# A nested Strassen–Winograd kernel on one core: PSUM as two tiles of two adjacent banks, and sums of seven blocks handled as wide operations

## The chip, the core and the metric

The kernel runs on one core of a Trainium2 chip. Its engines work side by side, each through its own instructions in order: TensorE (PE, matmuls, with the loading of the stationary operand shown apart as PEld), VectorE (DVE), ScalarE (ACT), GpSimd (POOL) and SyncE (SP, which here only issues DMAs). Matmuls write to PSUM, of which the kernel uses eight banks of 512 float32 numbers for each of 128 partitions. The metric is device time in microseconds (us), lower is better; 747.59 us is the median before the change.

## What is computed

Normalised linear attention in eight batches of eight heads, and a feed-forward block on its output:

```python
kv = np.einsum('bhsd,bhse->bhde', k, v)          # batch 8, heads 8, seq 576, head_dim 64
out = np.einsum('bhsd,bhde->bhse', q, kv)
rms = np.sqrt(np.mean(out * out, axis=-1, keepdims=True) + 1e-06)
attn = out / rms * g_norm
x = attn.transpose(0, 2, 1, 3).reshape(4608, 512)
a = x @ w1                                       # 512 x 1024
b = x @ w2
h = a * b @ w3                                   # 1024 x 1024
return h @ w_out                                 # 1024 x 512
```

## The kernel before

**Stages.** First w3 and w_out are multiplied into one 1024 x 512 matrix (`fold_chunk`, L678, four PSUM banks for a half), while weights arrive as 64-bit numbers and are turned into float32 (`conversion`). Then tokens are worked through in nine groups of 512: 512 tokens of a batch each, and one group (T = 8) of the 64 tokens left over from every batch; the order is T = 0 to 6, 8, 7. For a group there are the *gates* (x @ w1 and x @ w2, multiplied elementwise) and the *projection* by the folded matrix. The attention of batch T + 1 runs in pieces between products of group T: `between()` takes the next piece of `steps(b)`, which has eight lists of calls, and two `between()` are in each call of the gates, two in each half of the blocks. Where a piece has matmuls they are kv products (`begin_kv`, L335), the products with q (`finish` → `product`, L413, followed by `norm`, L374) and `product_left` (L432).

**Strassen–Winograd.** A product of 2 x 2 blocks is made with seven block products and some sums. `winograd` (L696) issues them in the order p1 (a11·b11), p5 (s1·t1), s2·t2 onto p1's bank (giving u2), s4·b22 onto p5's bank, s3·t3 onto the first bank (u3), a12·b21 into a third bank, a22·t4 onto the first. So three banks, r1, r2 and r3, serve seven products. What is needed later is kept in SBUF by a copy on ACT (`keep`, L717 to L719: p1, p5, u2, sometimes u3); the sums are finished on DVE by `done`: in the gates c12, c22 and c11 by an add (L848) and a multiplication (L849), c21 by a copy of one half on ACT (L843) and a multiplication with the other half in PSUM (L845). A product onto the bank of an earlier one waits until the earlier sum has been read.

**Two levels.** In T = 2 to 6, 8 and 7 (`IN_TWO`) the four 128-column parts p of the gates are split: p = 2 and p = 3 go by `gates` as above, p = 0 and 1 together by `gates_of_two` (L936), which has two halves w, each of seven products of seven blocks of 128 x 128; a sum of seven blocks takes two PSUM banks, four blocks in one and three in the other. There `keep` is two copies on ACT (L984, L985), `add` two adds on DVE (L989, L990), and `finish` (L1001 to L1006) four adds that turn seven blocks into a 2 x 2 result, and for w = 1 a multiplication with what w = 0 left. The projection of T ≥ 1 (`project_twice`, L1140) is built the same way, with `sum_inner` (L1125) making the inner sums of the left operand, four operations on 256 elements for each of the seven outer products. A call of the gates or of a half has seven products, and so has the projection (six and `last_block` in the last group).

**Order within a group of two levels.** `gates` for p = 2, `sum_ab(2)` (sums of the outputs for the projection), `gates_of_two`, two of the four operations of `sum_ab_two`, `gates` for p = 3 with the other two and `sum_inner(0)`, `sum_inner(1)` placed after its c22, c11 and c21 (`following`, L1448), and `project_twice`.

**Banks.** Five banks, `ps_mm`, are handed out in rotation: three to a call of `winograd`, five to `gates_of_two` (pairs named in `plan`), four to `project_twice`, sometimes one to attention; `ps_at` has three for transposes and attention.

**What sets the order.** PE, POOL and SP take their instructions in the order of the program (`manual_schedule`). DVE does so from the gates of p = 3 to the end of the projection, and in T = 8 and 7 (`TWICE`) from before `gates_of_two`. Elsewhere DVE, and ACT always after the first stage, get their order when the program is built, by a planner that follows program order as a priority and its own estimate of when inputs are ready. `tc.issue_after(x)` puts an instruction behind x; `run_slot` uses it to put ACT's copies for turning q and x (1.05 to 1.17 us each, L294, L296, L308) behind chosen `keep` copies. On SBUF the kept sums have tiles by name (p1, p5 and one for all u), and a new sum waits until the old one has been read.

## Time and profile before

| | us |
|---|---|
| median of 3 runs (746.46 to 747.67) | 747.59 |
| span of the profiled execution, first to last instruction | 744.3 |
| median of the runs less that span | 3.29 |
| PE busy, of the span | 736.6 |
| DVE busy | 648.0 |
| ACT busy | 379.3 |
| matmuls of `winograd`, 128 x 256, on the chain that ended last (L705) | 37% |
| matmuls of `project_twice`, 128 x 128 (L1175) | 23% |
| matmuls of `gates_of_two`, 128 x 128 (L964) | 21% |
| ACT copy out of PSUM, 128 x 512 | 0.586 |
| DVE add from PSUM, 128 x 512 (L989) | 0.68 |

The page of the profile has the span alone for the profiled execution; its whole time is not shown, so the difference to the median stands for what lies around it. Each line of the profile names engine, source line and tiles (out<-in). Matmul rows overlap: a row's duration is longer than the distance to the next matmul, so the pace is read from starts. "Pitch" below is the distance between the starts of two operations that follow each other on DVE or ACT; it is shorter than the duration, and longer when the second needs the first's result.

### The profile page before, as it was taken

How to read it: one execution, taken by the hardware profiler on the slowest of the kernel's cores; microseconds unless marked ns; L12 is line 12 of the kernel's file. 1: busy time of each engine (PE TensorE's matmuls, PEld its weight loads, DVE VectorE, ACT ScalarE, POOL GpSimd, SP SyncE). 2: the span in 40 equal slices, each digit the busy share in tenths (PEclk: the TensorE clock that was granted, in tenths of full speed). 3: DMA queues.
4: the chain of work that ended last, by engine and by line, in shares of the span. 5: the costliest groups of instructions: out<-in, count | busy, mean ns of one | idle time of the engine just before them, and what ended most of it. 6: DMA issues, size and time to landing. Idle time of an engine off the chain costs nothing.

```text
span 744.3 us, 16995 instructions
## 1 busy us (share of the span) xinstructions
PE 736.6 (99%) x6843; PEld 657.9 (88%) x6843; DVE 648.0 (87%) x1377; ACT 379.3 (51%) x652; POOL 22.4 (3%) x29
## 2 busy tenths in 40 slices
PE   8999999999999999999999999999999999999998
PEld 5455788888899999999999999999999999999997
DVE  7987998967869798989898989898989997898897
ACT  6787868415553575356536753575267323222421
POOL 0000000132000000010000000000001000000000
PEclk9999999999999999999999999999999999999999
DMA  9997934499997789678967896679757662465454
GB/s 316 367 304 220 256 103 126 122 337 301 285 294 291 213 221 274 264 200 244 276 237 208 255 291 243 213 240 264 254 141 220 215 217 87 163 227 163 135 198 136
DMA packets 135458, 169.67 MB, mean 228 GB/s; under 512 B 78036, under 2 KB 110804, under 8 KB 135380
## 3 DMA queue, kind: packets, MB, share of 16 engines
q1 hardware_dynamic: 132928, 154.16, 68.0%
q10 hardware_dynamic: 2452, 14.42, 5.6%
q8 instruction: 54, 0.88, 0.5%
q14 instruction: 24, 0.20, 0.1%
HBM read 130.55 MB, written 20.71 MB: 203 GB/s over the span
## 4 chain that ended last, share of the span: by engine, by line
PE 95%; DVE 2%; DMA 2%; ACT 0%; issue 0%; SPq 0%; ACTq 0%; DVEq 0%
PE mm L705 37%; PE mm L1175 23%; PE mm L964 21%; PE mm L682 7%; PE at L335 2%; PE at L413 1%; DMA raw<-in_moe_w_out_dram 1%; PE mm L413 1%; PE at L669 1%; DVE ab L162 1%; DVE w_sb L172 0%; PE at L1226 0%; DMA raw<-in_moe_w_dram 0%; DVE c L848 0%; PE at L432 0%
## 5 line engine op out<-in xcount | busy, mean ns | idle before, releaser
L705 PE MATMUL mm<-xT,w_sb 128*128 128x256 f32 x480 | 110.2, 379 | 0.0
L705 PEld LDWEIGHTS mm<-xT,w_sb 128*128 128x128 f32 x480 | 90.3, 190 | 12.2 <-issue 0.5
L705 PE MATMUL mm<-xc,ws 128*128 128x256 f32 x352 | 79.6, 379 | 0.0
L705 PEld LDWEIGHTS mm<-xc,ws 128*128 128x128 f32 x352 | 66.9, 190 | 9.1
L682 PE MATMUL mm<-chunks,ab 128*128 128x512 f32 x128 | 60.7, 605 | 0.7 <-DVE chunks L172 0.7
L964 PE MATMUL mm<-ws,w3o_sb 128*128 128x128 f32 x350 | 53.9, 275 | 0.0
L719 ACT COPY u<-mm 128x512 f32<-128x512 f32 x38 | 22.3, 586 | 58.0 <-PE mm L705 31.0
L1186 ACT COPY u<-mm 128x512 f32<-128x512 f32 x23 | 13.5, 586 | 75.3 <-DVE raw L1199 44.0
L1175 PE MATMUL mm<-w3o_sb,ab 128*128 128x128 f32 x368 | 48.6, 275 | 0.0
L719 ACT COPY p<-mm 128x512 f32<-128x512 f32 x46 | 27.0, 588 | 41.6 <-PE mm L705 26.6
L1175 PE MATMUL mm<-w3o_sb,raw 128*128 128x128 f32 x372 | 48.1, 275 | 0.0
L964 PEld LDWEIGHTS mm<-ws,w3o_sb 128*128 128x128 f32 x350 | 46.4, 192 | 0.0
L1175 PEld LDWEIGHTS mm<-w3o_sb,ab 128*128 128x128 f32 x368 | 45.4, 192 | 0.4
L1175 PEld LDWEIGHTS mm<-w3o_sb,raw 128*128 128x128 f32 x372 | 44.8, 192 | 0.0
L705 PE MATMUL mm<-xc,w_sb 128*128 128x256 f32 x176 | 42.5, 384 | 0.9 <-ACT u L719 0.9
L381 DVE TENSOR_REDUCE inv<-sq 128x8 f32<-128x512 f32 (+1 forms) x40 | 24.6, 629 | 21.1 <-ACT sq L380 21.1
L682 PEld LDWEIGHTS mm<-chunks,ab 128*128 128x128 f32 x128 | 21.6, 190 | 22.4 <-issue 14.4
L705 PE MATMUL mm<-xT,ws 128*128 128x256 f32 x160 | 38.5, 384 | 0.0
L705 PEld LDWEIGHTS mm<-xc,w_sb 128*128 128x128 f32 x176 | 32.7, 190 | 6.2 <-ACT u L719 1.7
L843 ACT COPY c<-mm 128x256 f32<-128x256 f32 x22 | 8.2, 371 | 53.9 <-PE mm L705 53.9
L308 ACT COPY xT<-xn 128x1024 uint16<-128x1024 uint16 x28 | 32.5, 1168 | 2.3 <-DMA xn<-xT 2.3
L705 PEld LDWEIGHTS mm<-xT,ws 128*128 128x128 f32 x160 | 29.8, 190 | 4.2
(250 smaller groups left out, 1745.9 us busy)
## 6 DMA issues: line engine op xcount, KB each, us to landing
w3o_sb<-w_l SPq DMA_DIRECT2D x21, 896.0 KB, 5.4
w3o_sb<-w3o_l SPq DMA_DIRECT2D x18, 896.0 KB, 5.1
raw<-in_moe_w_dram SPq DMA_DIRECT2D x31, 512.0 KB, 7.6
raw<-w3o_l SPq DMA_DIRECT2D x15, 896.0 KB, 4.7
w3o_sb<-w3o_l ACTq DMA_DIRECT2D x14, 896.0 KB, 5.0
k_sb<-in_k_dram SPq DMA_DIRECT2D x16, 576.0 KB, 4.7
v_sb<-in_v_dram SPq DMA_DIRECT2D x16, 576.0 KB, 5.9
q_sb<-in_q_dram SPq DMA_DIRECT2D x32, 256.0 KB, 3.5
```

Of the source, the lines that this page charges most:

```text
L162: nc.vector.scalar_tensor_tensor(out=low_bits, in0=hi, scalar=0x80000000, in1=low_bits, op0=ALU.bitwise_and, op1=ALU.bitwise_or,)
L308: copy(words(dst), src)
L335: nc.tensor.matmul(ps[r * D:(r + 1) * D, :], lhsT=k_sb[rows, r, cols], rhs=v_sb[rows, r, cols], start=(j == 0), stop=(j == JS - 1),)
L381: adds["norm"] = nc.vector.tensor_reduce(out=inv[:, i], in_=sq.rearrange("p (h d) -> p h d", d=D), axis=AX.X, op=ALU.add)
L413: nc.tensor.matmul(o_ps[l][tokens, n * D:(n + 1) * D], lhsT=qT[r][rows, e, i, tokens], rhs=kv_b[rows, m // 2 ^ l, e, h, :], start=True, st ...
L682: nc.tensor.matmul(sums_ps[half][m], lhsT=w3T[half, c][:, m, :], rhs=chunks[:, c, 1, :], start=(c == 0), stop=(c == KF - 1),)
L705: nc.tensor.matmul(ps[:, u, :], lhsT=lhsT(a_name, u, c), rhs=rhs(b_name, c),  start=(u == 0 and c == 0 and to is None), stop=(c == chunks ...
L719: copies.setdefault(name, []).append(nc.scalar.copy(t, ps))
L843: copied = nc.scalar.copy(c, one[:, 0, :])
L964: nc.tensor.matmul(ps[place // 4][:, place % 4, :], lhsT=x, rhs=y, start=new and place // 4 not in seen, stop=True, skip_group_check=True,)
L1175: nc.tensor.matmul(to[:, i, :], lhsT=x[:, c, :], rhs=y[:, c, :], start=new and place // 4 not in seen, stop=(c == 1), skip_group_check=True,)
L1186: nc.scalar.copy(t[:, 0:4], ps[0])
```

## The change

PSUM is now two tiles of two adjacent banks each, `mm`, for everything that used `ps_mm`, and four banks `ps_at`. Each call takes the next *unit*, 0 and 1 in turn: with unit u, `winograd` has r1 in the first bank of tile u, r2 and r3 in the two banks of the other tile; `gates_of_two` (a unit for each half) and `project_twice` have r1 = tile u and r2 = the other tile, whole.

Since a sum of seven blocks lies in adjacent banks, it is kept by one copy and added by one add of 896 elements. Kept sums lie in three *slots* of one tile; two of them that are neighbours are finished together by `finish_two_sums` (operations twice as wide, with a multiplication for each; `ab`'s two tiles are one, `ab_all`). In the second half of `gates_of_two` the slots are 2 (p1), 0 (u2), 1 (p5) and 2 (last). In `winograd` p5 takes slot 2, u2 and u3 slot 1, and p1 lies in a part of `pair_of_sums`, the tile that also has the inner sums of two outer products. `sum_inner` takes the products 1 and 2, and 5 and 6, in pairs. The sums of p = 2 for the projection join those of p = 0 and 1 (three parts instead of two) and come after `gates_of_two`; `sum_inner(1, 2)` and two sums of p = 3 come after c21. Pieces of attention move: the kv products of the batch after next by two places for batches from 3 on (from the gates of p = 3 to the third place of `gates_of_two`'s second half), and one end of turning q from behind u3 to behind u2 of the projection. In the projection (not the last) the add of p5 reads PSUM directly and u3 is no longer kept.

The diff, cut to its core:

```diff
@@ -74,8 +74,8 @@
-    ps_mm = ctx.enter_context(tc.tile_pool(name="ps_mm", bufs=5, space=PSUM))
-    ps_at = ctx.enter_context(tc.tile_pool(name="ps_at", bufs=3, space=PSUM))
+    ps_mm = ctx.enter_context(tc.tile_pool(name="ps_mm", bufs=1, space=PSUM))
+    ps_at = ctx.enter_context(tc.tile_pool(name="ps_at", bufs=4, space=PSUM))
@@ -83,6 +83,16 @@
+    mm = [ps_mm.tile([P, 2, 512], FP32, name=f"mm{i}") for i in range(2)]
+    units = []
+    def next_unit():
+        units.append(len(units) % 2)
+        return units[-1]
+    def two_banks(k):
+        return mm[k].rearrange("p b (i n) -> p (b i) n", n=P)
@@ -400,8 +411,7 @@
-            of_mm = b and not (h and b > FIRST_OF_TWO)
-            o_ps = [bank(*((ps_mm, "mm") if of_mm else (ps_at, "at"))), bank(ps_at, "at")]
+            o_ps = [bank(ps_at, "at") for _ in range(2)]
             for m in range(4):
@@ -568,7 +578,7 @@
                 at(("p3", "u2"), begin, ("q", b + 1, r), n.q_by_dma, r)
-                at(("proj", ("u2", "u3")[r]), end, ("q", b + 1, r))
+                at(("proj", "u2"), end, ("q", b + 1, r))
@@ -639,7 +649,7 @@
         if more:
-            fs[6 if in_two else second].append((batch(b + 1).begin_kv, 0))
+            fs[second].append((batch(b + 1).begin_kv, 0))
         fs[second].append((a.finish, 1))
@@ -690,16 +700,23 @@
-    def late_tile(name):
 ...
+    sums_in_slots = []
+    def late_slots(a, n=1):
+        return sums_in_slots[0][:, a] if n == 1 else sums_in_slots[0][:, a:a + n]
     def winograd(
 ...
     ):
-        def product(a_name, b_name, to=None):
-            ps = to if to is not None else bank(ps_mm, "mm").rearrange("p (u n) -> p u n", u=2)
+        unit = next_unit()
+        r1, r2, r3 = (
+            mm[k][:, i, :].rearrange("p (u n) -> p u n", u=2)
+            for k, i in ((unit, 0), (1 - unit, 0), (1 - unit, 1))
+        )
+        def product(a_name, b_name, ps, new=True):
             for u in range(2):
@@ -707,35 +724,38 @@
                         rhs=rhs(b_name, c),
-                        start=(u == 0 and c == 0 and to is None),
+                        start=(u == 0 and c == 0 and new),
                         stop=(c == chunks - 1),
 ...
             after()
 ...
         def keep(name, ps):
-            t = late_tile(name)[:, 0:4, :].rearrange("p (u a) n -> p u (a n)", u=2)
+            if name == "p1":
+                t = pair_of_sums[:, 0].rearrange("p s c t -> p (s c) t")
+            else:
+                t = late_slots(2 if name == "p5" else 1)
+            t = t[:, 0:4, :].rearrange("p (u a) n -> p u (a n)", u=2)
             copies.setdefault(name, []).append(nc.scalar.copy(t, ps))
 ...
             return t
-        r1 = product("a11", "b11")
+        product("a11", "b11", r1)
         p1 = keep("p1", r1)
-        r2 = product("s1", "t1")
+        product("s1", "t1", r2)
         p5 = keep("p5", r2)
-        product("s2", "t2", r1)
+        product("s2", "t2", r1, False)
         u2 = keep("u2", r1)
         between()
-        product("s4", "b22", r2)
+        product("s4", "b22", r2, False)
         done("c12", r2, u2)
-        product("s3", "t3", r1)
+        product("s3", "t3", r1, False)
         done("c22", p5, keep("u3", r1) if keep_u3 else r1)
-        r3 = product("a12", "b21")
+        product("a12", "b21", r3)
         done("c11", r3, p1)
         between()
-        product("a22", "t4", r1)
+        product("a22", "t4", r1, False)
         done("c21", r1, None)
@@ -935,9 +959,7 @@
     def gates_of_two(T, between=lambda: None):
-        mm = [bank(ps_mm, "mm").rearrange("p (i n) -> p i n", n=P) for _ in range(5)]
-        plan = [((0, 1), (2, 3), (4, 2)), ((3, 4), (2, 0), (1, 2))]
-        names = [("p1", "p5", "u2", "p1"), ("u2", "p5", "p1", "u2")]
+        places = [(0, 1, 2, 0), (2, 0, 1, 2)]
         def products(n, w, ps, new):
@@ -979,39 +1000,26 @@
-        def keep(name, ps, at):
-            t = late_tile(name)
-            nc.scalar.copy(t[:, 0:4], ps[0])
-            run_slot(at, nc.scalar.copy(t[:, 4:7], ps[1][:, 0:3]))
-            return t
+        def keep(slot, ps, at):
+            z = late_slots(slot)
+            run_slot(at, nc.scalar.copy(z, ps[:, 0:7]))
+            return z
         def add(z, ps):
-            nc.vector.tensor_add(z[:, 0:4], ps[0], z[:, 0:4])
-            nc.vector.tensor_add(z[:, 4:7], ps[1][:, 0:3], z[:, 4:7])
+            nc.vector.tensor_add(z, ps[:, 0:7], z)
         def finish(z, w, i, j):
 ...
+            finish_sums(z, ab[i][:, 0:2, j, :].rearrange("p m (n t) -> p m n t", t=P), w)
         for w in range(2):
-            r1, r3, r2 = ([mm[i] for i in pair] for pair in plan[w])
-            of_p1, of_u2, of_p5, of_last = names[w]
+            unit = next_unit()
+            r1, r2 = two_banks(unit), two_banks(1 - unit)
+            of_p1, of_u2, of_p5, of_last = places[w]
             products(0, w, r1, True)
             p1 = keep(of_p1, r1, (w, 0))
-            products(1, w, r3, True)
-            add(p1, r3)
+            products(1, w, r2, True)
+            add(p1, r2)
             finish(p1, w, 0, 0)
@@ -1019,17 +1027,50 @@
             add(p5, r1)
-            finish(p5, w, 1, 1)
             products(5, w, r2, False)
             add(z, r2)
-            finish(z, w, 0, 1)
+            both = ab_all[:, :, 0:2, 1, :].rearrange("p i m (n t) -> p i m n t", t=P)
+            finish_two_sums(late_slots(of_u2, 2), both, w)
             products(6, w, r1, False)
 ...
+    def finish_sums(z, dst, multiply=False):
+        def wide(i):
+            return z[:, i:i + 1].to_broadcast([P, 2, P])
+        to_0, to_1 = (z[:, m:m + 4:3] for m in range(2)) if multiply else (dst[:, m] for m in range(2))
+        nc.vector.tensor_add(z[:, 6], z[:, 6], z[:, 0])
+        nc.vector.tensor_add(z[:, 4:6], z[:, 4:6], wide(6))
+        nc.vector.tensor_add(to_1, z[:, 1:3], wide(4))
+        last = nc.vector.tensor_add(to_0, z[:, 3:6:2], z[:, 0:3:2])
+        if multiply:
+            made = z[:, 0:6].rearrange("p (n k) t -> p k n t", n=2)[:, 0:2]
+            last = nc.vector.tensor_mul(dst, dst, made)
+        return last
+    def finish_two_sums(z, dst, multiply=False):
+        def wide(i):
+            return z[:, :, i:i + 1].to_broadcast([P, 2, 2, P])
+        to_0, to_1 = (
+            (z[:, :, m:m + 4:3] for m in range(2)) if multiply else (dst[:, :, m] for m in range(2))
+        )
+        nc.vector.tensor_add(z[:, :, 6], z[:, :, 6], z[:, :, 0])
+        nc.vector.tensor_add(z[:, :, 4:6], z[:, :, 4:6], wide(6))
+        nc.vector.tensor_add(to_1, z[:, :, 1:3], wide(4))
+        last = nc.vector.tensor_add(to_0, z[:, :, 3:6:2], z[:, :, 0:3:2])
+        if multiply:
+            for i in range(2):
+                made = z[:, i, 0:6].rearrange("p (n k) t -> p k n t", n=2)[:, 0:2]
+                last = nc.vector.tensor_mul(dst[:, i], dst[:, i], made)
+        return last
     def sum_ab_two():
-        c11, c12, c21, c22 = (ab[i][:, 0:2, j, :] for i in range(2) for j in range(2))
-        s1, s2, s4 = (t[:, 0:2] for t in ab_sums)
+        c11, c12, c21, c22 = (ab[i][:, 0:NF - 1, j, :] for i in range(2) for j in range(2))
+        s1, s2, s4 = (t[:, 0:NF - 1] for t in ab_sums)
         return [
@@ -1122,20 +1163,34 @@
-    def sum_inner(n, between=lambda: None, place=None):
 ...
+    def sum_inner(*ns, between=lambda: None):
+        x_1 = ab[1].rearrange("p f j n -> p j f n")
+        if ns == (1, 2):
+            x = two_ab_sums[0]
+        elif ns == (5, 6):
+            x = x_1
+        else:
+            n, = ns
+            x = {0: ab[0][:, :, 0], 3: ab_sums[2], 4: ab[0][:, :, 1], 6: x_1[:, 1]}[n].unsqueeze(1)
         a11, a12, a21, a22 = (
-            x[:, 2 * j:2 * j + 2, i * P:(i + 1) * P] for i in range(2) for j in range(2)
+            x[:, :, 2 * j:2 * j + 2, i * P:(i + 1) * P] for i in range(2) for j in range(2)
         )
-        s1, s2, s4 = inner_sums[(n if place is None else place) % 3]
+        if len(ns) == 2:
+            s1, s2, s4 = (pair_of_sums[:, :, i] for i in range(3))
+        else:
+            s1, s2, s4 = (
+                t.unsqueeze(1) for t in (
+                    inner_sums[n % 4 // 3] if n < 6 else [pair_of_sums[:, 0, i] for i in range(3)]
+                )
+            )
         nc.vector.tensor_add(s1, a21, a22)
 ...
         nc.vector.tensor_sub(a21, a11, a21)
-        inner[n] = [a11, a12, a22, s1, s2, s4, a21]
+        for i, n in enumerate(ns):
+            inner[n] = [t[:, i] for t in (a11, a12, a22, s1, s2, s4, a21)]
@@ -1170,38 +1226,32 @@
             ):
-                to, i = ps[place // 4], place % 4
                 for c in range(2):
                     nc.tensor.matmul(
-                        to[:, i, :], lhsT=x[:, c, :], rhs=y[:, c, :],
+                        ps[:, place, :], lhsT=x[:, c, :], rhs=y[:, c, :],
                         start=new and place // 4 not in seen,
 ...
                     seen.add(place // 4)
 ...
         def keep(name, ps):
-            t = late_tile(name)
-            nc.scalar.copy(t[:, 0:4], ps[0])
-            run_slot(("proj", name), nc.scalar.copy(t[:, 4:7], ps[1][:, 0:3]))
-            return t
+            z = late_slots({"p1": 0, "p5": 2}.get(name, 1))
+            run_slot(("proj", name), nc.scalar.copy(z, ps[:, 0:7]))
+            return z
         def finish(z, half, j):
 ...
             dst = o_sbs[half][:, :, j * N:(j + 1) * N].rearrange("p m (i n) -> p m i n", n=P)
 ...
+            adds["out"] = finish_sums(z, dst)
             if not last:
-                if j == 0:
-                    store(half)
+                store(half)
             elif (half, j) != (0, 0):
                 store_block(half, j)
+        def finish_right():
+            dst = two_o_sbs[0][:, :, :, N:2 * N].rearrange("p h m (i n) -> p h m i n", n=P)
+            finish_two_sums(late_slots(1, 2), dst)
@@ -1252,31 +1300,29 @@
         if last:
-            sum_inner(6, place=5)
+            sum_inner(6)
             finish(p1, 0, 0)
             add(z, r2)
-        else:
-            add(z, r2)
-            sum_inner(5)
-        finish(z, 0, 1)
-        products(4, r1)
-        if last:
+            finish(z, 0, 1)
+            products(4, r1)
             add(p5, r1)
-        z = keep("u3", r1)
-        load_after()
-        if not last:
-            sum_inner(6)
-            nc.vector.tensor_add(p5, p5, z)
-        finish(p5, 1, 1)
-        products(6 if last else 5, r2)
-        load_after()
-        if last:
+            z = keep("u3", r1)
+            load_after()
+            finish(p5, 1, 1)
+            products(6, r2)
+            load_after()
             add(z, r2)
 ...
         else:
+            add(z, r2)
+            sum_inner(5, 6)
+            products(4, r1)
+            add(p5, r1)
+            load_after()
+            finish_right()
+            products(5, r2)
+            load_after()
             add(p1, r2)
@@ -1431,14 +1478,15 @@
             gates(T, p, between)
-            run(sum_ab(p))
             if T in TWICE:
 ...
             of_two = sum_ab_two()
-            for _ in range(2):
+            for _ in range(3):
                 of_two.pop(0)()
+        else:
+            of_two = []
@@ -1446,17 +1494,9 @@
                 following = {
-                    "c12": [], "c22": [sum_1],
-                    "c11": [
-                        lambda: sum_inner(0, lambda: all_of(f() for f in (sum_2, sum_3))),
-                        lambda: sum_inner(1),
-                    ],
-                    "c21": [sum_4],
+                    "c12": [], "c22": [sum_1], "c11": [lambda: sum_inner(0, between=sum_2)],
+                    "c21": [*of_two, lambda: sum_inner(1, 2), sum_3, sum_4],
                 }
-                if T in IN_TWO:
-                    following["c22"].append(of_two[0])
-                    following["c21"].append(of_two[1])
```

## The prediction

> **What bounds the kernel now.** I read the page first (shares and chain), then busy time by stretches, then the timelines of the places where the new bank order makes a product wait. The page says that the matmuls are the bound:
>
> ```profile
> span 744.3 us, 16995 instructions
> PE 736.6 (99%) x6843; PEld 657.9 (88%) x6843; DVE 648.0 (87%) x1377; ACT 379.3 (51%) x652; POOL 22.4 (3%) x29
> ...
> PE 95%; DVE 2%; DMA 2%; ACT 0%; issue 0%; SPq 0%; ACTq 0%; DVEq 0%
> ```
>
> Stretches that end at group boundaries (columns: length, then PE, PEld, DVE, ACT, POOL busy) show how full PE is:
>
> ```profile
> 82.00:163.00 81.00, 80.13 (x712) 68.95 (x712) 73.73 (x139) 47.80 (x80) 8.13 (x7) 1.00 0.58 170
> 363.00:437.00 74.00, 74.00 (x810) 70.02 (x809) 66.58 (x151) 41.76 (x74) 1.04 (x1) 1.00 0.80 244
> 650.00:718.00 68.00, 68.00 (x506) 65.11 (x505) 60.45 (x136) 18.60 (x35) 0.00 (x0) 1.00 0.53 175
> ```
>
> From the second group to the last PE has no hole at all; 82 to 163 has 0.9 us, two waits for ACT copies. The change leaves the matmuls alone, so whatever it saves on DVE and ACT can return about 1 us, while every new wait of PE is paid in full. The question is whether fewer free banks make new waits.
>
> **The pace.** By the starts of matmuls a product lasts 8 x 0.216 = 1.73 us in the gates (177.95 to 179.67 below), 14 x 0.112 = 1.57 us in the blocks, 28 x 0.112 = 3.14 us in the projection. PE resumes 0.05 us after the copy that frees its bank (copy 106.27 + 0.59, next matmul 106.91).
>
> **Step 1: the banks of c21.** Now the second product of a call writes the bank that the previous call's last product used; before it took another of the five. So it waits until c21 is read, by the ACT copy (L843) and the multiplication (L845), and has one product's time for it. In the seam from p = 0 to p = 1 of T = 1 the timeline of all engines says:
>
> ```profile
> 177.95 1.89 PE L705 MATMUL mm<-xT,w_sb 128*128 128x256 f32 x8
> 178.15 0.37 ACT L843 COPY c<-mm 128x256 f32<-128x256 f32 x1 [0.42 <-PE mm L705]
> 178.56 1.27 DVE L381 TENSOR_REDUCE inv<-sq 128x8 f32<-128x512 f32 x2
> 179.67 3.62 PE L705 MATMUL mm<-xc,ws 128*128 128x256 f32 x16
> ...
> 180.85 0.68 DVE L390 TENSOR_TENSOR xn<-mm,inv 128x512 f32<-128x512 f32 x1
> 181.45 0.68 DVE L390 TENSOR_TENSOR xn<-at,inv 128x512 f32<-128x512 f32 x1
> ...
> 182.71 0.42 DVE L845 TENSOR_TENSOR ab<-c,mm 128x256 f32<-128x256 f32 x1
> ```
>
> The second product starts at 179.67, the multiplication ends at 183.13: with the same DVE order PE waits 3.46 + 0.05 = 3.5. The same reading elsewhere: T = 0, p = 1 to 2, product 110.46, multiplication 111.82 + 0.42: 1.8. T = 0, p = 2 to 3, 125.83 against 126.77 + 0.41: 1.4. Gates p = 2 to the blocks in T = 2 to 6, 401.30 against 401.08 + 0.41: 0.25 each, five times, 1.2. The seam p = 3 to the projection in T = 0 (0.2 late) I count as nothing: DVE runs unbroken before it and gains the 3.2 us that PE has lost by then. Sum 7.9. The least it can be: the multiplication goes first once its copy is there. Then the first costs nothing (178.52 + 0.42 is before 179.67), the second still 1.4 (copy ends 111.36, behind two conversions on ACT), the third 0.1, the fourth nothing: 1.5. I take 7.9, since the work ahead of it (the norm, the sums of the weights) stands ahead of it in the program too.
>
> **Step 2: the end of the blocks.** In the second half the last product's sum now lies in slot 2, and so does p5 of the gates that follow. p5's copy must wait for that sum's last multiplication, and the gates' fourth product, which adds to the same bank, for the copy. Before it was u2 that met the last sum, and its bank is needed one product later. Before, in T = 7 (DVE, then ACT, then PE):
>
> ```profile
> 703.55 0.56 DVE L990 TENSOR_TENSOR p<-mm,p 128x384 f32<-128x384 f32 x1
> ...
> 710.48 0.43 DVE L1003 TENSOR_TENSOR c<-u 128x256 f32<-128x256 f32 x1
> 710.83 0.42 DVE L1004 TENSOR_TENSOR c<-u 128x256 f32<-128x256 f32 x1
> 711.28 0.69 DVE L1006 TENSOR_TENSOR ab<-ab,c 128x512 f32<-128x512 f32 x1
> ```
>
> ```profile
> 710.06 0.59 ACT L719 COPY p<-mm 128x512 f32<-128x512 f32 x1 [1.14 <-PE mm L705]
> 711.83 0.59 ACT L719 COPY u<-mm 128x512 f32<-128x512 f32 x1 [1.18 <-PE mm L705]
> ```
>
> ```profile
> 711.58 1.89 PE L705 MATMUL mm<-xT,ws 128*128 128x256 f32 x8
> ```
>
> After: the sixth product ends at 705.0 and its wide add of 896 starts at 705.1. No row reads two banks at once; the parts bound it, 0.68 + 0.55 above, and their slope (1.02 ns an element) gives 1.07, an SBUF add of 896 took 1.08 (L1271). I take 1.08. Then in order, a dependent step starting 0.03 after its source ends: 256, 512, 512, 512 elements and two multiplications of 512 by pitches 0.46, 0.72, 0.60, 0.72, 0.60, 0.60, to 709.9; the last sum 0.32, 0.46, 0.34, 0.46 and 0.69, to 712.2. Copy of p5 0.59, to 712.85; PE at 712.9 instead of 711.58: 1.3 in each of T = 8 and 7, where DVE goes in program order. In T = 2 to 6 the order is the planner's, and it weaves the two finishes together (before, at 425 to 428, pitches of 0.20 to 0.34 instead of 0.46), 0.5 less: 0.8. Least 0.3; most 2.3, if the norm's three operations (0.24 and twice 0.69, 422 to 424) fall between the add and the finish. Moving the next batch's kv from the gates into the blocks takes away the 1.2 us (429.01 to 430.22) that lay ahead of that fourth product, and that is in these bounds: measured from the sixth product T = 2 to 5 now look like T = 7. Sum 2 x 1.3 + 5 x 0.8 = 6.6, bounds 3.1 and 14.1. Behind the waiting copy ACT holds turning copies of 1.05 each; behind PE's product everything.
>
> **Step 3: slot 2 in the blocks.** The first kept sum of the second half waits for the first half's double finish. T = 7: add 694.16 to 695.24, four wide operations to 697.75, copy of 896 (slope of 0.586 at 512 and 0.371 at 256: 0.91) to 698.7, third product due 698.59. 0.15 with the resumption, seven times, 1.0; bounds 0 and 1.5.
>
> **Edits at nothing.** *Two banks read at once:* a block product's read must now fit into one product, 1.57 less 0.17 to its start, against 0.91 on ACT or 1.08 on DVE: 0.3 left, gone only where the engine is late, which are steps 1 to 3. *Sums of the projection:* sums 1 and 2 now come after c21. From c11's read, ready at 361.97 as its last matmul ends at 361.87, by the pitches at 363 to 370: multiplication of c21 done 365.5, s4 of three chunks 366.3, wide sums done 367.0, 367.7, 368.4, 369.0; the second product (366.57) needs them at 367.9, 368.4, 368.8, 369.3. It fits by 0.3; without that, 0.3 in each of eight groups. At the end the sixth product's read lands near 384.5, due 385.31 (before 385.81, in other banks). *p = 2's sums* leave 397 to 402 and ride with the two others, 0.27 an operation, behind step 2 in a DVE that then idles 0.9 (432.30). *kv of the next batch:* its 72 matmuls take the same PE time; six ACT copies at 0.22 come behind u2's; its two loads on SP pass the turning transposes and the loads of w3o parts, needed only in the next group, some 40 us on. *End of q by ACT:* one copy of 1.17 and one load of q move from u3 to u2, into an ACT gap of 6.1. *The at banks, four for three:* transposes and kv do not wait for banks today. *DVE saved:* some 30 instructions a group, about 0.1 each by pitch (0.60 for 512 against twice 0.34, or 0.72 against twice 0.46), 3 us of 73, hidden under PE.
>
> The Trainium skill, Perfetto Trace Analysis, section Optimizing Scalar/DVE Operations, weighs against this change: larger operations help a saturated engine, but where Scalar or Vector are not saturated and cause bubbles elsewhere, breaking instructions up may end work sooner. It puts the overhead that a DVE instruction on PSUM saves at about 125 ns; three adds saved in each of 14 halves would be 5 us of DVE by that, where the pitches (1.18 for the pair, about 1.0 for one) give 8; of the time the sum takes neither, as PE is full.
>
> **Sum.** 7.9 + 6.6 + 1.0 = 15.5. Span 744.3 + 15.5 = 759.8. The profiled execution's whole time is not shown; the median of the runs, 747.59, lies 3.3 above its span, so 763.
>
> **Rivals.**
> - *The order on DVE follows the new waits* (c21 first, finishes woven): 1.5 + 3.1 + 0 = 4.6, 752. For it: outside T = 7 and 8 the order is the planner's. Against: c21 stands late because norm and sums are ahead in the program.
> - *No loss, a small gain:* the lighter DVE comes early at every seam, so no new wait holds, and the two ACT waits at 106 and 121 (0.37 and 0.83 beyond the pace) go: 746.4. It decides if the finish ends 6.4 us or less after the sixth product; by step 2 it takes 7.1, and the copy after it.
> - *DVE becomes the bound* at the end of the blocks, norm inside: 7.9 + 14.1 + 1.5 = 23.5, 771.
>
> **How the numbers follow.** Forecast 0.52 (756 to 768, around 763), order follows 0.22 (749.5 to 756), no loss 0.12, DVE bound 0.14 (768 to 776). Range 749.5 to 773: it leaves out the no-loss case and the end of the worst. 0.2% (1.5 us) is about what a measurement of this kernel can tell. No loss splits into faster 0.05 and the same 0.07; slower 0.88.
>
> **What would show it.** Right: in the chain and the waits, PE L705 waiting for DVE's L845 line (3 us near 180) and for ACT's p5 copy in the gates after the blocks, that copy waiting for DVE's last multiplication; 1 to 2 us between the groups' starts more than before; busy DVE lower. Wrong: PE still 68.0 of 68.0 in the late groups (step 2 false), or no hole before 200 us (step 1). It would be most wrong if the planner reorders DVE, or if slots and banks wait more coarsely than by the piece that is touched, which would add waits at every product.

## The result and the profile after

The changed kernel takes 792.0 us (median of four runs, 789.74 to 792.26) against 747.03 for the kernel before in the same comparison: 1.0594 times as long, 95% interval 1.0579 to 1.061. The direction was forecast, the size was not: 45 us in place of 15.5. The profiled execution took 789.74 us with a span of 788.0, which is 43.7 more than the 744.3 of before.

The page of after, its span, busy times, the shares of the chain that ended last, and the two wide operations (count, busy time, mean ns of one, idle time ahead of them):

```profile
span 788.0 us, 16523 instructions
...
PE 747.5 (95%) x6843; PEld 659.3 (84%) x6843; DVE 631.4 (80%) x1146; ACT 362.1 (46%) x550; POOL 21.4 (3%) x29
...
PE 61%; DVE 9%; ACT 6%; issue 1%; DMA 1%; ACTq 0%; SPq 0%; DVEq 0%
...
L1005 ACT COPY slots<-mm 128x896 f32<-128x896 f32 x56 | 50.7, 905 | 51.2 <-PE mm L986 29.5
L1009 DVE TENSOR_TENSOR slots<-mm,slots 128x896 f32<-128x896 f32 x42 | 45.5, 1083 | 25.9 <-PE mm L986 25.9
```

DVE and ACT did become lighter, by 16.6 and 17.2 us of busy time, and the wide reads cost what the prediction took for them (0.905 and 1.083 us against 0.91 and 1.08). But PE, which had 95% of the chain, has 61%. The view of waits for PE (us in total, times, longest) names what it waits for; before, its largest entry past the start-up was 0.9 us:

```profile
PE mm L722 <- ACT slots L739: 12.1, 7, 2.1
PE mm L722 <- DVE slots L1009: 6.3, 5, 1.3
PE mm L722 <- DVE c L872: 6.3, 6, 1.7
PE mm L692 <- ACT w3o_sb L697: 3.2, 4, 1.4
PE mm L722 <- DVE ab L869: 2.1, 1, 2.1
...
PE mm L1230 <- DMA w3o_sb<-w3o_l: 1.3, 1, 1.3
```

L722 is `winograd`'s matmul (L705 before), L739 its `keep`, L1009 the blocks' `add`, L872 and L869 the gates' add and c21's multiplication, L692 and L697 the fold's matmul and its copy out of PSUM. A wait below is given as the distance between the starts of two matmuls less the usual pace, which is some 0.16 more than the time shown here.

**Where the loss lies.** The matmuls are the same 6843 in the same order of products, so the loss can be read stage by stage, from the starts of the same matmul in the two traces. All runs of this study, in us of span beyond before's 744.3 (one profiled execution each):

| | to the gates of T = 0 | gates of T = 0, 1 | projection of T = 1 | T = 2 to 6 | T = 8, 7 | sum | median (us) |
|---|---|---|---|---|---|---|---|
| after | 4.5 | 9.5 | 1.5 | 24.8 | 3.4 | 43.7 | 792.0 |
| e1_p5_apart | 4.5 | 11.9 | 1.9 | 11.7 | 1.8 | 31.7 | 777.0 |
| e2_kv_back | 4.2 | 9.6 | 1.7 | 20.9 | 3.4 | 39.8 | 786.4 |
| e3_single_banks | 0.3 | 8.3 | 2.7 | 24.7 | 3.4 | 39.3 | 786.8 |
| e4_all_three | 0.5 | 8.3 | 4.1 | 13.3 | 1.8 | 27.9 | 774.1 |
| e5_norm_behind_add | 0.0 | 11.3 | 2.1 | 6.6 | 1.8 | 21.8 | 766.8 |
| e6_banks_in_turn | 0.5 | 2.1 | 1.2 | 13.3 | 1.8 | 18.8 | 765.8 |
| e7_all_five | 0.6 | 2.1 | 2.1 | 6.7 | 1.8 | 13.1 | 759.2 |
| e8_finish_apart | 4.6 | 11.2 | 2.5 | 19.9 | 5.4 | 43.5 | 788.3 |
| e9_narrow | 4.5 | 11.2 | 2.9 | 16.2 | 3.8 | 38.6 | 784.4 |
| e10_norm_alone | 4.7 | 11.2 | 1.6 | 29.6 | 3.4 | 50.5 | 794.5 |
| e11_before_kv | 0.4 | 0.1 | 0.0 | 2.4 | 0.0 | 2.8 | 749.5 |
| e12_five_narrow | 0.9 | 2.0 | 1.6 | 7.8 | 2.3 | 14.6 | 761.6 |

A wait before the first product of a stage counts in the stage ahead of it. About 1.7 us of a cell come from a stretch of half clock on PE (last section) where one fell there: in the gates of T = 0, 1 of e1, e5, e8, e9 and e10, in the projection of T = 1 of e3 and e4, in T = 2 to 6 of after, e3 and e8, and five times in T = 2 to 6 of e10 (once twice as long).

**T = 2 to 6** lose most, and nearly all of it at one place, from the end of the blocks to the fourth product of the next gates call. Here it is in T = 3, from the timeline of all engines (start, duration, engine, line; in brackets the idle time before and its releaser):

```profile
368.50 2.20 ACT L319 COPY xT<-xn 128x1024 uint16<-128x1024 uint16 x2
...
368.80 1.03 DVE L1009 TENSOR_TENSOR slots<-mm,slots 128x896 f32<-128x896 f32 x1
...
370.74 1.29 DVE L401 TENSOR_TENSOR xn<-at,inv 128x512 f32<-128x512 f32 x2 [0.91 <-ACT xT L319]
...
371.94 1.08 DVE L1009 TENSOR_TENSOR slots<-mm,slots 128x896 f32<-128x896 f32 x1
...
373.08 1.13 PE L722 MATMUL mm<-xT,w_sb 128*128 128x256 f32 x4 [1.30 <-DVE slots L1009]
```

The sixth product of the blocks is done by about 370.3, but its add (the second L1009) stands on DVE behind the norm's two multiplications (L401), and these wait 0.91 us for ACT's turning copies to let go of the tile xn. Before, this lateness cost nothing: the next gates call took a bank of its own. Now it takes the pair which that add reads, and PE stands until 373.08, 1.47 us. What follows on DVE is late as well:

```profile
377.28 0.42 DVE L1047 TENSOR_TENSOR slots<-slots 128x256 f32<-128x256 f32 x1
377.62 0.95 DVE L1075 TENSOR_TENSOR raw<-ab 128x768 f32<-128x768 f32 x1
378.49 0.68 DVE L1050 TENSOR_TENSOR ab<-ab,slots 128x512 f32<-128x512 f32 x1
378.56 0.58 ACT L739 COPY slots<-mm 128x512 f32<-128x512 f32 x1 [1.92 <-DVE raw L1075]
379.05 1.05 ACT L307 COPY qT<-q_sb 128x1024 uint16<-128x1024 uint16 x1
...
379.99 0.59 ACT L739 COPY slots<-mm 128x512 f32<-128x512 f32 x1
...
380.63 0.70 PE L722 MATMUL mm<-xT,ws 128*128 128x256 f32 x2 [2.11 <-ACT slots L739]
```

The last multiplication of the blocks (L1050), which frees slot 2 for p5, comes behind a sum of the projection (L1075) that the planner put in between. ACT's order has changed too: u2's copy (378.56) and a turning copy of 1.05 us now stand ahead of p5's copy (379.99). The fourth product, due at 378.36, starts at 380.63: 2.27 us. In T = 8 and 7, where DVE takes the program's order and there is no norm, this wait is 1.33.

**The gates of T = 0 and 1, and the fold,** wait for readers of another bank. The timeline of after at p = 1 of T = 0:

```profile
108.98 1.89 PE L722 MATMUL mm<-xT,w_sb 128*128 128x256 f32 x8
...
110.70 0.68 DVE L872 TENSOR_TENSOR c<-mm,slots 128x512 f32<-128x512 f32 x1
...
111.44 0.92 PE L722 MATMUL mm<-xT,w_sb 128*128 128x256 f32 x3 [0.57 <-DVE c L872]
```

The product at 111.44 is a12·b21, which goes into the second bank of its pair. That bank was last read in the fold. The add at 110.70 is c12's and reads the first bank, and PE starts 0.06 us after its end. In the same way the first product of p = 1 starts at 100.56, 0.06 us after the end of c11's add (99.82 + 0.68), which reads the other bank of the pair that the product writes. The reading, which e3 tests below: a wait is kept for the whole tile, and a tile is now two banks.

### The profile page after: what moved, and what is told of

Read it like the earlier page. It is cut to its first block, busy times and chain, and to the rows that moved or that the text cites. A ratio compares the mean times of both kernels' runs of the same rounds, so it can differ in the third digit from the quotient of the medians.

```text
span 788.0 us, 16523 instructions
## 1 busy us (share of the span) xinstructions
PE 747.5 (95%) x6843; PEld 659.3 (84%) x6843; DVE 631.4 (80%) x1146; ACT 362.1 (46%) x550; POOL 21.4 (3%) x29
## 4 chain that ended last, share of the span: by engine, by line
PE 61%; DVE 9%; ACT 6%; issue 1%; DMA 1%; ACTq 0%; SPq 0%; DVEq 0%
PE mm L722 24%; PE mm L1230 21%; PE mm L986 14%; PE at L346 2%; DVE inv L392 2%; ACT sq L391 2%; ACT xT L319 1%; ACT kv_sb L356 1%; ACT slots L739 1%; DVE xn L401 1%; DVE slots L1009 1%; DMA w3o_sb<-w3o_l 1%; DVE ab L1068 1%; DVE raw L1075 1%; ACT slots L1005 0%
## 5 line engine op out<-in xcount | busy, mean ns | idle before, releaser
L722 PE MATMUL mm<-xT,w_sb 128*128 128x256 f32 x480 | 111.9, 382 | 12.6 <-DVE slots L1009 6.3
L722 PEld LDWEIGHTS mm<-xT,w_sb 128*128 128x128 f32 x480 | 89.6, 190 | 28.5 <-DVE c L872 9.2
L1240 ACT COPY slots<-mm 128x896 f32<-128x896 f32 x32 | 29.0, 905 | 122.6 <-PE mm L1230 115.2
L722 PE MATMUL mm<-xc,ws 128*128 128x256 f32 x352 | 79.8, 380 | 2.1 <-DVE ab L869 2.1
L722 PEld LDWEIGHTS mm<-xc,ws 128*128 128x128 f32 x352 | 66.5, 190 | 11.9 <-ACT qT L307 2.5
L739 ACT COPY slots<-mm 128x512 f32<-128x512 f32 x61 | 35.5, 585 | 84.2 <-PE mm L722 62.3
L1005 ACT COPY slots<-mm 128x896 f32<-128x896 f32 x56 | 50.7, 905 | 51.2 <-PE mm L986 29.5
L1009 DVE TENSOR_TENSOR slots<-mm,slots 128x896 f32<-128x896 f32 x42 | 45.5, 1083 | 25.9 <-PE mm L986 25.9
L692 PE MATMUL mm<-chunks,ab 128*128 128x512 f32 x128 | 61.2, 607 | 4.4 <-ACT w3o_sb L697 3.2
L722 PE MATMUL mm<-xT,ws 128*128 128x256 f32 x160 | 40.4, 397 | 11.0 <-ACT slots L739 11.0
L722 PEld LDWEIGHTS mm<-xT,ws 128*128 128x128 f32 x160 | 30.7, 196 | 17.6 <-ACT slots L739 13.4
L692 PEld LDWEIGHTS mm<-chunks,ab 128*128 128x128 f32 x128 | 21.5, 190 | 27.0 <-issue 13.6
L1230 PE MATMUL mm<-w3o_sb,raw 128*128 128x128 f32 x340 | 43.5, 275 | 0.0
L722 PE MATMUL mm<-xc,w_sb 128*128 128x256 f32 x176 | 42.3, 383 | 0.0
L1230 PEld LDWEIGHTS mm<-w3o_sb,raw 128*128 128x128 f32 x340 | 40.7, 192 | 0.0
L722 PEld LDWEIGHTS mm<-xc,w_sb 128*128 128x128 f32 x176 | 32.9, 190 | 4.7
```

Source lines behind the costliest of these rows:

```text
L692: nc.tensor.matmul(sums_ps[half][m], lhsT=w3T[half, c][:, m, :], rhs=chunks[:, c, 1, :], start=(c == 0), stop=(c == KF - 1),)
L722: nc.tensor.matmul(ps[:, u, :], lhsT=lhsT(a_name, u, c), rhs=rhs(b_name, c),  start=(u == 0 and c == 0 and new), stop=(c == chunks - 1), s ...
L739: copies.setdefault(name, []).append(nc.scalar.copy(t, ps))
L1005: run_slot(at, nc.scalar.copy(z, ps[:, 0:7]))
L1009: nc.vector.tensor_add(z, ps[:, 0:7], z)
L1230: nc.tensor.matmul(ps[:, place, :], lhsT=x[:, c, :], rhs=y[:, c, :], start=new and place // 4 not in seen, stop=(c == 1), skip_group_check ...
```

## The experiments

The theory that they test has four parts: (a) slot 2 holds p5's copy back; (b) waits go by tile and not by bank; (c) the second product of a gates call waits for c21, as the prediction's step 1 said; (d) the norm stands ahead of an add that has become urgent. The rivals are the prediction's own reading (waits by bank, kv at nothing) and, for each part, that ACT and DVE are simply late, so that a wait taken away comes back elsewhere.

### p5's copy in a place of its own

From T = 2 on (`apart` is set there):

```diff
+            elif name == "p5" and apart:
+                t = pair_of_sums[:, 1].rearrange("p s c t -> p (s c) t")
```

> The kernel after, but from T = 2 on the p5 copy of a gates call goes into the second half of the tile inner_sums, which nothing else uses at that time, in place of slot 2 of the three slots. Theory (the wait is for the place in SBUF: p5's copy may not overwrite slot 2 before the last finish of the blocks has read it, and PE's fourth product waits for the copy): the waits of 2.27 us before the fourth product in T = 2 to 5, 1.54 in T = 6 and 1.33 in T = 7 and 8 go, 13.3 us, and some 0.1 us of slow start after each, so about 778 us against 792. Rival (the copy is late because the ScalarE queue is full of turning copies and the VectorE queue runs late, and the place is only where it shows): 0.8 us or more of each wait stays in T = 2 to 6, so 783 us or more.

Measured 777.0 us (1.0401, interval 1.0381 to 1.042): 15 less than after. T = 2 to 6 fell from 24.8 to 11.7 us and T = 8, 7 from 3.4 to 1.8; no wait for `keep`'s copy is left in the trace. In T = 8 and 7 a new wait of 0.5 us shows in its stead, for an add of c (a12·b21 and the neighbouring bank again), the two that the first line has more than after:

```profile
PE mm L722 <- DVE c L874: 7.4, 8, 1.7
PE mm L722 <- DVE slots L1011: 6.3, 5, 1.3
```

Part (a) is right: it was the place.

### kv back to the gates of p = 3

```diff
-            fs[second].append((batch(b + 1).begin_kv, 0))
+            fs[6 if in_two else second].append((batch(b + 1).begin_kv, 0))
```

> The kernel after, with the kv products of the next batch back where they were before the change (among the gates products of p = 3, not in the second half of the blocks). Theory (the six kv copies, 1.3 us of ScalarE, stand ahead of the squares of the norm; the norm's multiplications come that much later and stand on VectorE ahead of the add of the second kept sum, which now holds the banks of the next gates call): the wait of 1.47 us before the first product of p = 3 goes in T = 2 to 5, 5.9 us, and the VectorE work behind it ends earlier too, so that up to 1.45 us of the next wait goes in each, another 5.8 us: 780 to 786 us against 792. Rival (the move costs nothing, as the prediction had it, and the norm stands ahead of the add wherever kv is): 791 to 793 us. T = 6, which has no kv and still waited 1.47 us, speaks for the rival.

Measured 786.4 us (1.0529, 1.0512 to 1.0546): 5.6 less than after, but not by the way foreseen. The wait before the first product is still there (1.47, 1.35, 1.47, 1.35, 1.47), so the norm stands ahead of the add wherever kv is. What shrank is the wait before the fourth product in T = 2 to 5, from 2.27 to 1.01, because kv's matmuls lie ahead of that product again and fill 1.26 of it. In T = 2:

```profile
300.59 1.28 PE L346 MATMUL at<-v_sb,k_sb 64*64 64x64 f32 x72
...
302.13 0.59 ACT L739 COPY slots<-mm 128x512 f32<-128x512 f32 x1
...
302.77 1.99 PE L722 MATMUL mm<-xT,ws 128*128 128x256 f32 x8 [0.90 <-ACT slots L739]
```

p5's copy is no earlier: it starts 6.92 us after the call's first product, in after 6.91. In return come waits of 0.8 to 1.0 for a kept copy of the blocks and for a weight transfer, and the shared passage of kv and q is given up (last section).

### The four banks as four tiles in the first part

The pairs are made at the projection of T = 1:

```diff
+    one = [ps_one.tile([P, 512], FP32, name=f"one{i}") for i in range(4)]
+    def mm_bank(k, i):
+        return mm[k][:, i, :] if mm else one[2 * k + i]
...
+        if T and not mm:
+            single_cm.__exit__(None, None, None)
+            mm.extend(ps_mm.tile([P, 2, 512], FP32, name=f"mm{i}") for i in range(2))
```

> The kernel after, but until the second projection the same four banks are four tiles of one bank each, used in the same order; from then on two tiles of two banks as before. Theory (a wait is kept for a whole tile: a product into one bank of a pair waits for a reader of the other bank): in the fold 3.4 us of waits for the copies of sums go (1.6, 0.76, 1.07; the 0.4 for a bank's own copy stays), and in the gates of T = 0 and T = 1 the six waits for adds that read the neighbouring bank (1.25, 0.74, 1.25, 1.86, 0.84, 1.32, together 7.3 us): about 781 us against 792; the 2.3 us wait for c21's multiplication in T = 1, which reads the very bank, stays. Rival (waits are kept by bank, as the prediction had it, and these waits come of the order of the banks and of late adds): no change, 791 to 793 us.

Measured 786.8 us (1.0536, 1.0513 to 1.0558): 5.2 less, half of what was expected. The waits of PE say why:

```profile
PE one L727 <- DVE ab L874: 5.3, 3, 2.4
PE mm L1235 <- DVE ab L874: 1.9, 1, 1.9
...
PE one L727 <- ACT slots L744: 0.9, 2, 0.7
```

The fold's waits are gone, 4.5 us to 0.3, and so are all six waits for adds in a neighbouring bank: (b) is right. In their place stand waits for c21's multiplication, which reads the very bank: 1.83 and 1.41 in T = 0 and 2.54 in T = 1. In after the wait for the neighbour came a product earlier and gave c21 the time it needed. And the projection of T = 1 now waits 2.06 us for the pairs to be made from the single banks.

### The three together

> The three edits together. If the three causes are what they are taken for and do not overlap much: 792 less 14 (p5's place), less 6 (kv), less 10.7 (single banks) is about 761 us, and the 14 us that are left over the kernel before are the multiplication of c21 in T = 1 (2.3), the wait for a weight transfer in T = 1's projection (1.4), some 0.9 us in each of T = 2 to 6 and smaller things. If the waits only change their place (the next holder of the banks or of VectorE is late by as much): 770 us or more.

The edits are the three above. Measured 774.1 us (1.0365, 1.0348 to 1.0383), 13 more than hoped. 8.3 us are left in the gates of T = 0 and 1, of which the three c21 waits are 5.8 and the wait for the pairs, ahead of the projection of T = 1, is 2.1; 13.3 in T = 2 to 6, of which the five waits before the first product of p = 3 are 7.1. The next two experiments take these two.

### The norm behind the add

In T = 2 to 6 the norm is held after its squares, sums and square root, and ends here:

```diff
-            add(z, r2)
+            added = add(z, r2)
+            if w and held:
+                with tc.issue_after(added.ins):
+                    all_of(held.pop())
```

> The kernel of e4_all_three (p5's copy in a place of its own, kv back, single banks in the first part), and in T = 2 to 6 the norm's two multiplications are issued behind the add of the second kept sum in the second half of the blocks, where before they stood ahead of it on VectorE. Theory (VectorE is held by the norm, whose multiplications wait for ScalarE's turning copies to let go of the tile xn, and the add behind them is what frees the pair of banks for the next gates call): the five waits before the first product of p = 3 (1.47, 1.34, 1.47, 1.35, 1.47, together 7.1 us) go, with 0.1 us of slow start each: about 766.5 us against 774.1. Rival (VectorE and ScalarE are full at the end of the blocks, so what is freed there is missing a few us later, for the copy of p5 or the adds of p = 3): 771 us or more.

Measured 766.8 us (1.0263, 1.0241 to 1.0285) against 766.5 by the theory. The five waits are gone; T = 2 to 6 went from 13.3 to 6.6 us. Its profile lost 3 us more in T = 1, to a longer wait and a slow clock (last section).

### The banks in turn

```diff
+        if not mm:
+            turn = (len(units) - 1) % 3
+            banks = [one[n] for n in ((0, 2, 3), (1, 2, 0), (3, 2, 1))[turn]]
```

> The kernel of e4_all_three, and in the first part (T = 0 and the gates of T = 1), where the four banks are tiles of their own, the three banks of a call are chosen so that neither its first nor its second product writes a bank that the call before still reads for c21: the first product takes the bank that the call before left alone. Theory (the second product waits for c21's multiplication, which reads the same bank, as the prediction's first step had it): the waits of 1.83, 1.41 and 2.54 us go, and the 0.36 and 0.83 behind them, 7 us, so about 767 us against 774.1; the 2.06 us before the second projection stays, since the pairs are made anew there. Rival (ScalarE and VectorE are late in these stages whatever bank is taken, and the next bank is waited for instead): 772 us or more.

Measured 765.8 us (1.0248, 1.0232 to 1.0263) against 767. The three waits for c21 are gone and nothing took their place: 8.3 us became 2.1, which is the wait for the pairs. The 0.36 and 0.83 that were taken for their followers stayed; they are waits for ACT copies which the kernel before has too.

### All of it

> The edits of e5_norm_behind_add and e6_banks_in_turn together on the kernel of e4_all_three. If both causes are right and independent: 774.1 less 7.6 less 7 is 759.5 us; what is then left over the kernel before (12 us) is the change of the pairs and a late weight transfer at the second projection (4), the end of the blocks in T = 2 to 6 (0.6 to 1.6 each) and 0.9 each in T = 7 and 8. If a wait comes back in another place: 763 us or more.

Measured 759.2 us (1.0158, 1.0143 to 1.0173) against 759.5: the causes add up. The waits that are left:

```profile
PE mm L1002 <- ACT slots L1021: 2.2, 3, 0.8
PE mm L1249 <- DVE ab L885: 1.9, 1, 1.9
PE mm L1249 <- DMA w3o_sb<-w3o_l: 1.8, 1, 1.8
PE mm L736 <- DVE c L888: 1.4, 3, 0.7
```

The sum is met a little by luck: the two results by themselves, 7.3 and 8.3 less than e4, would have made 758.5. Of 43.7 us of span 13.1 remain: 6.7 in T = 2 to 6, 2 for the new pairs and 2 for a weight transfer at the projection of T = 1, 1.8 in T = 8 and 7. Each is a wait that the kernel before does not have, and with PE full there the saved work of DVE and ACT has nothing to give: no experiment pointed to a version below 747.

### The double finish undone

```diff
             add(p5, r1)
+            finish(p5, w, 1, 1)
             products(5, w, r2, False)
             add(z, r2)
-            finish_two_sums(late_slots(of_u2, 2), both, w)
+            finish(z, w, 0, 1)
```

> The kernel after, with the double finish of the blocks undone: p5 and the second kept sum are finished each by itself, p5 before the sixth product, as in the kernel before; banks, places and all else as after. Theory (the double finish, 2.4 us of adds and 1.4 of multiplications, ends in a heap with the last finish, and undoing it takes 1.4 us from behind the add of the second kept sum): in T = 7 and 8 the wait of 1.33 us before the fourth product goes; in T = 2 to 6 p5's own finish now stands ahead of that add, which comes 0.8 us later and makes the wait before the first product 2.3 us in place of 1.47, while the fourth product's wait shrinks by 0.7 or less: 789 to 795 us against 792. Rival (the double finish is the main cause of the late last finish everywhere): the fourth product's wait goes to 0.8 us or less in T = 2 to 6 too, 782 us.

Measured 788.3 us (1.0552, 1.0511 to 1.0593; its four runs spread over 6 us), just below the theory's range and far from the rival's 782. The wait before the fourth product went to 0.5 in T = 3 to 6, as low as the rival had it, and to nothing in T = 8 and 7; but that before the first product rose to 2.0 to 2.1 in T = 2 to 6 and, which was not foreseen, from nothing to 1.60 in T = 8 and 7, with another 0.87 in their blocks. So undoing the double finish takes 4.9 us from T = 2 to 6 and adds 2.0 in T = 8 and 7: it mostly moves the load from one wait to the other.

### The wide reads made narrow

```diff
-            run_slot(at, nc.scalar.copy(z, ps[:, 0:7]))
+            nc.scalar.copy(z[:, 0:4], ps[:, 0:4])
+            run_slot(at, nc.scalar.copy(z[:, 4:7], ps[:, 4:7]))
...
-            nc.vector.tensor_add(z, ps[:, 0:7], z)
+            nc.vector.tensor_add(z[:, 0:4], ps[:, 0:4], z[:, 0:4])
+            nc.vector.tensor_add(z[:, 4:7], ps[:, 4:7], z[:, 4:7])
```

> The kernel after with its wide reads of products made narrow again: each kept sum of the blocks and of the projections is copied by two instructions (four and three blocks) and added by two, in the banks and places of after. By the rows, a kept copy takes 0.58 and 0.48 us with 0.08 between them in place of 0.905, an add 0.69 and 0.56 in place of 1.08, so 0.15 to 0.25 us more on each engine for each. Theory (with the pairs, VectorE and ScalarE stand on the way to PE at the end of the blocks, so the wide forms now save time): each of the waits before the first and the fourth product of p = 3 grows by 0.15 to 0.4 us, in T = 2 to 8: 794 to 797 us against 792. Rival (the wide forms are worth nothing to PE, as the prediction had their savings hidden): 791 to 793 us.

Measured 784.4 us (1.0506, 1.0476 to 1.0535): 7.6 less than after. Both theories missed; more and smaller operations were faster. DVE in T = 3, from the timeline:

```profile
372.07 0.69 DVE L1010 TENSOR_TENSOR slots<-mm,slots 128x512 f32<-128x512 f32 x1 [0.42 <-PE mm L986]
372.68 1.28 DVE L401 TENSOR_TENSOR xn<-at,inv 128x512 f32<-128x512 f32 x2
373.87 0.55 DVE L1011 TENSOR_TENSOR slots<-mm,slots 128x384 f32<-128x384 f32 x1
...
379.19 0.68 DVE L1052 TENSOR_TENSOR ab<-ab,slots 128x512 f32<-128x512 f32 x1
379.79 0.95 DVE L1077 TENSOR_TENSOR raw<-ab 128x768 f32<-128x768 f32 x1
```

The first part of the add now runs ahead of the norm, in the time in which DVE stood idle for it, and only 0.55 us is left behind it: the wait is 1.04 in place of 1.47. The planner's order behind it is another one as well, the last multiplication (L1052) ahead of the sum for the projection (L1077), and p5's copy on ACT ahead of the turning copies, so the fourth product waits 0.86 in place of 2.27. T = 8 and 7, whose order is fixed, did not gain (3.8 against 3.4). The Trainium skill has this case in Perfetto Trace Analysis, section Optimizing Scalar/DVE Operations: where Scalar or Vector are not saturated but cause bubbles on other engines, breaking instructions up may end work sooner. The trace agrees in T = 2 to 6, though only in part by the splitting itself: of the 8.6 us there, the wait before the first product gave 2.0, the wait before the fourth 6.3, where the order changed too, and 1.7 is the half clock in T = 4 of after; some smaller waits grew.

### The norm alone

> The kernel after with one edit alone: in T = 2 to 6 the norm's multiplications behind the add of the second kept sum. Theory (two waits in a row for one heap of VectorE work: the add comes in time and the five waits of 1.3 to 1.47 us go, but the norm then lies between that add and the last finish, slot 2 comes free hardly earlier, and the wait for p5's copy grows by most of what was won): the first wait goes, the fourth product's wait is 2.8 us or more in place of 2.27: 786 to 790 us against 792. Rival (the late add holds up all that comes behind it, and with it on time both waits shrink): 777 us.

The edit is that of e5, on after and without the others. Measured 794.5 us (1.0632, 1.0592 to 1.0672): less of a gain still than the theory had, a loss. The five waits before the first product are gone; the wait for p5's copy is all the longer, 3.22 in place of 2.27 in T = 2 to 5 and 2.62 in place of 1.54 in T = 6, and a stretch of half clock (last section) comes with each:

```profile
PE mm L730 <- ACT slots L747: 17.0, 7, 3.1
```

By the waits alone the edit gains 2.3 us, as the theory had it; the half clock costs some 9.7 us in T = 2 to 6 against 1.7 in after, and makes a loss of it. On e4 the same edit is worth 7.3 us: it pays in full only once slot 2 is out of the way.

### kv moved in the kernel before

```diff
-            fs[6 if in_two else second].append((batch(b + 1).begin_kv, 0))
+            fs[second].append((batch(b + 1).begin_kv, 0))
```

> The kernel before with one edit: the kv products of the next batch in the second half of the blocks, where after has them. Theory (the place of kv costs something only because the pair and slot 2 have made the end of the blocks a matter of PE's time; in the kernel before nothing waits there): 746 to 749 us against 747.4. Rival (its six ScalarE copies are late for p5's copy and the norm by themselves): 1.2 us or more in each of T = 2 to 5, so 752 us or more.

Measured 749.5 us (1.0034, 1.0023 to 1.0045), between the two. PE waits for ACT at the q products, 0.66 us in each of T = 2 to 5:

```profile
PE at L413 <- ACT kv_sb L345: 2.6, 4, 0.7
```

kv and q in one place need four banks for attention, and before there are three there. Nothing of it reaches p5's copy or the norm.

### All of it, narrow

> The kernel of e7_all_five with the wide reads of products made narrow as in e9_narrow. In e9 the narrow form was 7.6 us faster than after. Theory (an add in two parts won there because its first part fits into VectorE's wait ahead of the norm, and because the last multiplication and the copy of p5 then stood ahead of other work; with the norm behind the add and p5 in a place of its own there is nothing of that left to win): 758.5 to 761 us against 759.15, no gain, some tenths of loss where a pair is read under a wait (0.2 us each before the products of T = 2, 4 and 6 that already wait 0.8). Rival (parts are better in themselves, since a bank's first half is read sooner): 757 us or less.

The edits of e7 and e9. Measured 761.6 us (1.0195, 1.0178 to 1.0212), 2.4 more than e7 and a little over the theory's range. With the order set right the narrow form loses: the wait before the third product of the second half (step 3 of the prediction) grows by 0.1 to 0.2 us in every group, and some others by as little. So the wide operations are worth some 2 us here (1.5 by the two profiles, both at a clock of 1.00; 2.4 by the medians, with clocks of 0.997 and 0.998 in three runs of e12), and in after they cost 5 by the spans and 8 by the medians, mostly through the order that came with them.

## Why the prediction missed

| step, as predicted | said | measured |
|---|---|---|
| 1: c21, T = 1, p = 0 to 1 | 3.5 | 2.3 in after; 2.5, 2.6, 3.4 in e3, e4, e5 |
| 1: c21, T = 0, two seams | 1.8 and 1.4 | none in after; 1.83 and 1.41 in e3 |
| 1: gates p = 2 to the blocks | 5 x 0.25 | 5 x 0.24 |
| 2: fourth product, T = 8 and 7 | 2 x 1.3 | 2 x 1.33 |
| 2: the same, T = 2 to 6 | 5 x 0.8 | 4 x 2.27 and 1.54 |
| 2: kv gone from ahead of it, T = 2 to 5, in the bounds | 1.2 | 1.26 (e2) |
| 3: slot 2, third product of the second half | 7 x 0.15 | 0.09 in T = 2, 4, 6; 0.17 in T = 3, 5, 8, 7 |
| "the fold" | not costed | 4.1 |
| add of z, first product of p = 3 | not costed as a wait | 4 x 1.47 and 1.30 |
| adds in a neighbouring bank, T = 0, 1 | not costed | six waits, 7.3 |

**Step 1 was right in mechanism and, where the waits go by bank, nearly in size** (5.8 us in e3 and e4 against 6.7). It was overtaken by what the prediction had named as its weak point and given no price: waits kept more coarsely than by the piece touched. The whole-tile waits cost 4.1 us in the fold, which the prediction left out entirely, and 7.3 in the gates of T = 0 and 1; since they come ahead of c21's they replace two of its three waits, so that the gates of T = 0 and 1 lost 9.5 in place of 6.7. The clue was there: `mm` is allocated as two tiles, and the prediction took the bank as the unit because the code's r1, r2 and r3 are banks.

**Step 2 failed in T = 2 to 6,** the largest miss, 17.8 us of waits (7.2 and 10.6) in place of 4.0. Two terms of it were wrong. First, it followed only the path of slot 2 and not that of the pair: the add behind the norm frees the banks of the next call's first product. The row that shows the norm ahead of it (422 to 424) was in the prediction's hands, but as a bound on the finish. Second, "the planner weaves the two finishes together, 0.5 less" was taken from the old order; the new program got a new order, with a sum for the projection ahead of the last multiplication and u2's copy and a turning copy ahead of p5's, on ACT. The 2.27 that came lies at the upper bound of 2.3, but by luck: that bound has the norm between the add and the finish, and the norm stood ahead of both. Kv's move was no part of the failure: its 1.2 us were in the bounds, and e2 gives 1.26. The lower bound of 3.1 for the step does not follow from its terms (2 x 1.3 + 5 x 0.3 is 4.1), so the first rival should have stood at 753. In T = 8 and 7, where the order is the program's, the working gave 1.3 and the trace 1.33; step 3 came out as worked.

**Edits at nothing.** The two-bank reads cost what was estimated, the projection's sums fit (no wait at the later projections), DVE's saving is hidden. *Kv at nothing* and *the at banks at nothing* hang together: with three banks (e11) the move of kv costs 2.8 us, with four it gives 0.25 us in each of T = 2 to 4, while q in T = 5 waited 0.95 (last section). A late weight transfer at the projection of T = 1 (1.43 us) was not costed. Of the rivals, *DVE becomes the bound* at the end of the blocks, norm inside, was nearest in mechanism; its 771 lacked the tile waits and the first product's wait. The range of 749.5 to 773 had room only for costs that had been found.

**What remains open:** why the planner chose the order it did; only its effect was measured. The half clock took 1.7 us of after's profiled run, and perhaps 3 in the others (granted clock 0.997 against 0.995 and 0.996, worked out below); it was not tried apart.

## What to carry to other kernels

When a buffer becomes part of a larger tile, cost its waits by the tile: list for each writer the last reader of any part, not of its own part. Where a planner sets the order, an old trace's order is no evidence for the new program; the terms that rest on it need the whole range between the best and the worst order, while stages with a fixed order can be worked out to a tenth. And one repair can show nothing until another is made (e10 against e5): take several causes away together before one is called harmless.

## What was not expected of the hardware

**A wait of two microseconds can halve PE's clock.** In T = 4 of after the matmuls behind the 2.27 us wait take twice their time. Windows of after, columns as in the prediction, the granted clock third from the end:

```profile
458.70:462.20 3.50, 3.41 (x8) 2.78 (x9) 0.37 (x1) 1.93 (x3) 0.00 (x0) 0.53 0.33 75
462.20:466.00 3.80, 3.80 (x19) 3.27 (x19) 2.69 (x6) 0.00 (x0) 0.00 (x0) 0.99 0.92 207
```

Eight matmuls at a pitch of 0.427 in place of 0.216 us: 1.7 us lost on top of the wait. Over the twelve profiles with pairs, past 100 us, it came with none of some 140 waits of 0.7 to 1.8 us, 9 of 39 from 1.8 to 2.4, and 6 of 9 that were longer, and cost 1.6 to 3.0 us each time. As far as these traces show, what decides is where the wait falls. In the traces' clock records each of these stretches begins a whole number of steps of 3.413 us after the start of the record (133 in after) and lasts one step, once two (e10). In the step ahead of each, PE was without matmuls for 2.06 us or more, by their starts and the usual pace; of the other steps past 100 us none had more than 2.11. So a wait of 2.27 us halves the clock only if nearly all of it falls into one step. The kernel before has no wait over 0.83 there, and e6 and e7, which have at most two over 1.9, run at 1.00 (one run of e6 at 0.998). The runs of after, e8 and e10, with granted clocks that change from run to run, spread by 2.5 to 6 us, those of e7 by 0.6. A mean clock of 0.995 over 790 us is 7.9 us at half speed, so at most 4 us of a run, an estimate from these figures; a half clock behind the last matmul counts in the mean and costs nothing (in after's profile 1.4 of 4.8 us). The Trainium skill, TensorE: Matmul & The Clock Gate (Why this matters for your kernels), advises against idle gaps of more than about 3 us; here gaps of 2.1 were enough at times, and the slow stretch of 3.41 us agrees with the window that its Part 1 states.

**Kv and q products that follow each other save PE time where there are banks enough.** In T = 2 to 4 of after, with four banks, they take 2.35 us from the matmul before to the matmul after; apart, in the kernel before, 1.52 and 1.30, in which a matmul of 0.22 counts that is not in the 2.35: 0.25 saved. Together in three banks (e11) they take 3.32, with waits for ACT's copies. In T = 5 of after they take 3.51; what q waits for there the profile does not show.
